# Two PSUM tiles for the halves of an expert's first product, and half an expert's weights loaded ahead of the gathers

## The chip, the cores and the metric

One core of a Trainium2 chip runs the kernel. The metric is the device time of one execution in microseconds. A core has five engines with queues of their own: TensorE (PE in the profile; its weight loads are PEld), VectorE (DVE), ScalarE (ACT), GpSimd (POOL) and SyncE (SP). Sixteen DMA engines move data between HBM and the on-chip memory SBUF. They take work from several queues: q1 is fed by SyncE, q0 by GpSimd. PSUM is the memory that TensorE writes its products to[...].

## The reference

Eight batches of attention with local and global tokens give an array x of 4352 rows and 512 columns. A mixture of experts follows: each row goes to the expert with the largest gate logit, each of eight experts keeps at most 80 rows, those with the largest gates, and only those rows of the output are not zero.

```python
x = np.ascontiguousarray(attn_out.transpose(0, 2, 1, 3)).reshape(B * S, H * D)
...
logits = x @ w_gate
expert_idx = np.argmax(logits, axis=1)
...
for e in range(E):                       # E = 8, D = 512, F = 1024
    tok_idx = np.where(expert_idx == e)[0]
    if len(tok_idx) > capacity:          # capacity = 80
        gw = gate_w[tok_idx]
        tok_idx = tok_idx[np.argpartition(-gw, capacity)[:capacity]]
    h = np.maximum(x[tok_idx] @ w1[e], 0.0)
    out[tok_idx] = gate_w[tok_idx, None] * (h @ w2[e])
```

## The kernel before

The program has a hand-written order on every engine. It runs in three stages.

**Attention.** A loop over sixteen half batches (`q`, L670) computes the attention and writes x, in bf16 and with each row's gate beside it, to the DRAM tensor `x_scr`. SyncE issues those writes (`Ld`, L553). Weights of the experts are loaded on the way by GpSimd, which converts them from fp32 to bf16 in the transfer. `load_w(e, parts)` (L606) loads an expert's weights in four parts of 512 KB as written: parts 0 and 1 are the two halves of the first matrix `w1sb`, parts 2 and 3 those of the second, `w2sb`. Experts 0 to 4 and half of expert 5 are issued inside the loop. `NRES` is 3, so `NRES + 2` is expert 5, `NRES + 3` is 6 and `NRES + 4` is 7.

**Routing.** After the loop SyncE writes the zeros of the whole output (`zeros`, L623, 17 pieces of 512 KB). Then comes, on GpSimd, the rest of expert 5's weights (L815). VectorE finds each expert's threshold and from it the list `idx` of the rows to keep (L876). TensorE runs matmuls that nobody reads meanwhile (`warm`, L635). Then GpSimd issues eight indirect gathers, one per expert, that fetch the kept rows from `x_scr` into `xg` (L880), and behind them, in its queue, the weights of experts 6 and 7 (L883).

**Experts.** For each expert (L924) TensorE does, in this order: four transposes of the next expert's gathered rows (`fx`, L888); the first product of this expert (`fh`, L896), in two halves of 16 matmuls each; the second product of the expert before (`fy`, L907), 8 matmuls of 512 columns. ScalarE empties each half of the first product with a relu (L905). VectorE and ScalarE each scale a half of the second product with the gates, and GpSimd scatters the 80 rows to the output (L917).

In `fh` both halves are written to one PSUM tile from `psO`:

```python
def psO(name):
    return ps.tile([P, 2, 512], FP32, tag="O", bufs=2, name=name)
...
h2_ps = psO(f"h_ps{e}")
for half in range(2):
    h_ps = h2_ps[:, half, 0:4 * cap].rearrange("p (f j) -> p f j", f=4)
```

Such a tile is two banks wide, and half 0 lies in the first bank, half 1 in the second. There are two buffers under the tag "O". The framework adds waits between engines by tile: a write to a tile waits for earlier reads of it.

Of the kernel before, what the change touches and what calls it, by code (L numbers as in the profile page):

```python
# [23 lines left out]
NRES = 3  # L24
# [56 lines left out]
def kernel(  # L81
# [18 lines left out]
    E = moe_w_gate.shape[1]  # L100
# [5 lines left out]
    cap = int(moe_capacity)  # L106
# [20 lines left out]
    def psO(name):  # L127
        return ps.tile([P, 2, 512], FP32, tag="O", bufs=2, name=name)
# [477 lines left out]
    def load_w(e, parts):  # L606
        for k in parts:
            if k < 2:
                nc.gpsimd.dma_start(out=w1sb[e][:, 2 * k:2 * k + 2],
                                    in_=moe_w1[e, 256 * k:256 * k + 256].rearrange("(c p) f -> p c f", p=P))  # L610
            else:
                k -= 2
                nc.gpsimd.dma_start(out=w2sb[e][:, 4 * k:4 * k + 4],
                                    in_=moe_w2[e, 512 * k:512 * k + 512].rearrange("(p c) f -> p c f", c=4))
# [20 lines left out]
    def warm(n):  # L635

        w_ps = psS([P, 512], FP32, "w_ps")
        for _ in range(n):
            nc.tensor.matmul(out=w_ps[:], lhsT=onesb[:], rhs=w1sb[0][:, 0, 0:512], start=True, stop=True)  # L639
# [30 lines left out]
    for q in range(NQ):  # L670
# [95 lines left out]
        if q < 4 * NRES:  # L766
            e, k = divmod(q, 4)
# [43 lines left out]
    for e in range(NRES + 2, E):  # L811
        if e > NRES + 2:
            w1sb[e] = w2pool.tile([P, 4, FF], BF16, name=f"w1sb{e}")
        w2sb[e] = w2pool.tile([P, 8, DF], BF16, name=f"w2sb{e}")
    load_w(NRES + 2, (2, 3))  # L815
    rpool = ctx.enter_context(tc.tile_pool(name="route", bufs=1, reuse_waits="tile"))
    xg = [rpool.tile([cap, XW], FP32, name=f"xg{e}") for e in range(E)]
    for e in range(E):
# [60 lines left out]
    for e in range(E):  # L879
        nc.gpsimd.indirect_dma_start(out=xg[e][:], out_offset=None, in_=x_dram.ap(),  # L880
                                     in_offset=bass.IndirectOffsetOnAxis(ap=idx[:, e:e + 1], axis=0),
                                     bounds_check=N - 1, oob_is_err=False)
    for e in range(NRES + 3, E):  # L883
        load_w(e, (0, 1, 2, 3))
    warm(16)
    xTs, hTs = {}, {}

# [7 lines left out]

    def fh(e):  # L896
        hTs[e] = rpool.tile([P, 8, cap], BF16, tag="fhT", bufs=2, name=f"fhT{e}")
        h2_ps = psO(f"h_ps{e}")
        for half in range(2):
            h_ps = h2_ps[:, half, 0:4 * cap].rearrange("p (f j) -> p f j", f=4)  # L900
            for f in range(4):
                for cc in range(4):
                    nc.tensor.matmul(out=h_ps[:, f, :], lhsT=w1sb[e][:, cc, 512 * half + f:512 * half + 512:4], rhs=xTs[e][:, cc, :],
                                     start=(cc == 0), stop=(cc == 3))
            nc.scalar.activation(out=hTs[e][:, 4 * half:4 * half + 4, :], in_=h_ps, func=AF.Relu, scale=1.0)  # L905
# [18 lines left out]
    for e in range(E):  # L924
        if e + 1 < E:
            fx(e + 1)
        fh(e)
        if e:
            fy(e - 1)
# [37 lines left out]
```

The softmax here doesn't subtract the row's maximum and nothing guards it: scores larger than these inputs give would overflow.

## Time and profile before

| | us |
|---|---|
| median of 3 runs | 281.66 |
| lowest, highest | 279.4, 283.12 |
| span of the profiled execution | 281.7 |
| TensorE busy | 232.1 |
| first gather issued by GpSimd | 230.18 |
| first transpose of gathered rows | 236.78 |
| last scatter issued | 275.86 |

The page gives, for the whole span, the busy time of each engine, then the span in 40 slices, the DMA queues, a chain of waits and the costliest groups of instructions. Each instruction carries the line of the kernel that it comes from. For a change in one stage the answers of the trace by window tell more than the page: who waited for whom between two times, the instructions in order of time, and the DMA queues' share in that stretch. In a timeline line the first number is the start, the second how long the row lasts, then engine, line, operation, out<-in and shapes; in square brackets stand the idle time ahead of it and what ended it. Three slices' worth of numbers of the page frame the stage in question: the memory traffic between 211 and 239 us is 236 to 418 GB/s, between 239 and 268 us 144 to 214, and 47 after that.

### The profile page before, as it was taken

How to read it: one execution, taken by the hardware profiler on the slowest of the kernel's cores; microseconds unless marked ns; L12 is line 12 of the kernel's file. 1: busy time of each engine (PE TensorE's matmuls, PEld its weight loads, DVE VectorE, ACT ScalarE, POOL GpSimd, SP SyncE). 2: the span in 40 equal slices, each digit the busy share in tenths (PEclk: the TensorE clock that was granted, in tenths of full speed). 3: DMA queues.
4: the chain of work that ended last, by engine and by line, in shares of the span. 5: the costliest groups of instructions: out<-in, count | busy, mean ns of one | idle time of the engine just before them, and what ended most of it. 6: DMA issues, size and time to landing. Idle time of an engine off the chain costs nothing.

```text
span 281.7 us, 9676 instructions
## 1 busy us (share of the span) xinstructions
PE 232.1 (82%) x4029; PEld 161.6 (57%) x4029; DVE 146.3 (52%) x450; ACT 137.5 (49%) x238; POOL 158.6 (56%) x215
## 2 busy tenths in 40 slices
PE   8776649999999999999998999979779792598880
PEld 3355537677577676676676677658234352455550
DVE  2647404454554467769168576696879740011210
ACT  3637058669569569569568576450500000123230
POOL 6719409668677776786683987884600027812221
PEclk9999658999999999999999999997999996589998
DMA  7899598969789899999999889969999999899511
GB/s 244 213 299 196 125 342 209 246 189 201 159 215 247 146 254 244 197 261 198 182 261 196 228 164 163 221 122 171 292 273 236 324 418 387 154 213 214 144 47 47
DMA packets 70924, 60.85 MB, mean 216 GB/s; under 512 B 49248, under 2 KB 53600, under 8 KB 70880
## 3 DMA queue, kind: packets, MB, share of 16 engines
q1 hardware_dynamic: 62608, 41.01, 51.5%
q0 software_dynamic: 7840, 18.80, 37.1%
q8 instruction: 31, 0.51, 0.8%
q10 hardware_dynamic: 432, 0.43, 0.4%
q14 instruction: 13, 0.11, 0.1%
HBM read 62.35 MB, written 14.70 MB: 273 GB/s over the span
## 4 chain that ended last, share of the span: by engine, by line
PE 31%; DMA 25%; issue 13%; DVE 10%; ACT 8%; POOL 6%; SPq 4%; POOLq 1%; ACTq 0%; DVEq 0%
PE o_ps L408 7%; DMA x_scr<-xgb 6%; DMA out_dram<-zt 5%; DMA qkb<-in_k_l_dram 5%; PE o_ps L395 5%; DVE xn L416 4%; PE T_ps L308 4%; ACT qkT L311 4%; DMA w1sb<-in_q_g_dram 4%; PE x_ps L443 3%; PE og L427 3%; PE lt_ps L465 3%; DMA vg<-in_v_g_dram 3%; ACT eL L366 2%; POOL out_dram L917 2%
## 5 line engine op out<-in xcount | busy, mean ns | idle before, releaser
L374 POOL TENSOR_TENSOR eL<-eL,band 128x512 f32<-128x512 f32 x30 | 38.8, 1293 | 36.3 <-ACT eL L366 36.2
L311 ACT COPY qkT<-T_ps 128x1024 f16<-128x1024 f16 x32 | 32.5, 1018 | 34.5 <-PE T_ps L308 29.9
L408 PE MATMUL o_ps<-vb,eL 128*64 128x65 f32 x1024 | 45.3, 234 | 0.0
L408 PEld LDWEIGHTS o_ps<-vb,eL 128*64 128x64 f32 x1024 | 36.5, 143 | 9.9 <-issue 6.0
L366 ACT ACTIVATE eL<-l_ps 128x512 f32<-128x512 f32 x64 | 34.9, 600 | 13.9 <-PE l_ps L361 13.9
L158 ACT CAST qkr<-qkb 128x1024 f16<-128x1024 f32 x27 | 28.7, 1064 | 9.6 <-DMA qkb<-in_q_l_dram 8.6
L905 ACT ACTIVATE fhT<-h_ps 128x320 bf16<-128x320 f32 x16 | 6.9, 432 | 48.8 <-remote 37.8
L443 PE MATMUL x_ps<-misc,xn 128*128 128x128 f32 x128 | 20.9, 286 | 8.3 <-DVE xn L416 8.3
L308 PE MATMUL T_ps<-ident,qkr 128*128 128x128 f16 x256 | 21.2, 229 | 7.1 <-ACT qkr L158 5.6
L320 POOL COPY kO<-qkT 128x512 f16<-128x512 f16 x31 | 18.5, 623 | 13.3 <-ACT eg L509 6.8
L639 PE MATMUL w_ps<-w1sb,onesb 128*128 128x512 bf16 x110 | 25.1, 379 | 0.0
L880 POOL DMA_INDIRECT xg<-x_scr,idx x8 | 7.8, 973 | 28.3 <-DMA out_dram<-zt 26.2
L416 DVE TENSOR_TENSOR xn<-o_ps,rec 128x512 f32<-128x512 f32 x32 | 22.1, 692 | 2.1
L415 DVE RECIPROCAL rec<-o_ps 128x8 f32<-128x8 f32 x32 | 6.5, 204 | 32.0 <-PE o_ps L408 32.0
L308 PEld LDWEIGHTS <-qkr 128*128 128x128 f16 x256 | 15.3, 102 | 10.9 <-ACT qkr L158 6.9
L917 POOL DMA_INDIRECT out_dram<-y,idx x8 | 7.4, 930 | 24.0 <-ACT y L915 24.0
L395 PE MATMUL o_ps<-vg,eG 32*128 32x65 f32 x512 | 19.8, 277 | 0.3 <-DMA vg<-in_v_g_dram 0.2
L443 PEld LDWEIGHTS x_ps<-misc,xn 128*128 128x128 f32 x128 | 13.4, 140 | 11.4 <-DVE xn L416 7.3
L454 POOL CAST xb<-xn 128x1024 bf16<-128x1024 f32 x16 | 16.6, 1036 | 4.5 <-DVE xn L416 4.5
L395 PEld LDWEIGHTS o_ps<-vg,eG 32*128 32x128 f32 x512 | 17.2, 186 | 3.3 <-issue 2.2
L224 POOL COPY vb<-vb 64x1040 f32<-64x1040 f32 x16 | 16.7, 1045 | 3.5 <-DMA vb<-in_v_l_dram 3.5
L225 POOL COPY vb<-vb 64x1040 f32<-64x1040 f32 x16 | 17.2, 1077 | 0.9
(148 smaller groups left out, 445.2 us busy)
## 6 DMA issues: line engine op xcount, KB each, us to landing
out_dram<-zt SPq DMA_DIRECT2D x17, 512.0 KB, 9.2
qkb<-in_q_l_dram SPq DMA_DIRECT2D x16, 512.0 KB, 5.8
qkb<-in_k_l_dram SPq DMA_DIRECT2D x16, 512.0 KB, 6.4
vb<-in_v_l_dram SPq DMA_DIRECT2D x48, 128.0 KB, 5.6
w2sb<-in_moe_w_dram POOLq DMA_DIRECT2D x12, 512.0 KB
w1sb<-in_moe_w_dram POOLq DMA_DIRECT2D x10, 512.0 KB
x_scr<-xb SPq DMA_DIRECT2D x8, 514.0 KB, 5.4
vb<-in_moe_w_dram POOLq DMA_DIRECT2D x6, 512.0 KB
```

Of the source, the lines that this page charges most:

```text
L158: cp(out=qkr[q][:, t].rearrange("p i g d -> p g i d"), in_=qkb[q % 2][:, t])
L225: nc.gpsimd.tensor_copy(out=v[64:128, 5:9], in_=v[64:128, 0:4])
L308: nc.tensor.transpose(out=T_ps[:, i].rearrange("x a p -> x (a p)"), in_=qkr[q][:, t, i].rearrange("p g d -> p (g d)"), identity=ident16[:, :])
L311: cp(out=dst, in_=T_ps[:].rearrange("x i a p -> x a p i"))
L320: (nc.gpsimd if q or a else nc.vector).tensor_copy(out=kO[q % 2][:, a], in_=qkT[q % 2][:, a, 576:1088].rearrange("x (u w y) -> x u w y", w ...
L366: nc.scalar.activation(out=eL[:], in_=l_ps[hh][:], func=AF.Exp, scale=scale)
L374: eng.tensor_tensor(out=eL[:], in0=eL[:], in1=band[:].rearrange("p t i -> p (t i)"), op=ALU.mult)
L395: nc.tensor.matmul(out=s["o"][h][:, u, :], lhsT=s["eG"][32 * r:32 * r + 32, 128 * u:128 * u + 128], rhs=vg[b % 2][32 * r:32 * r + 32, qd, ...
L408: nc.tensor.matmul(out=o[64 * odd:64 * odd + 64, u, :], lhsT=s["eL"][h][:, 64 * t:64 * t + 64], rhs=v[:, 5 * odd + u, h, :], start=False, ...
L416: nc.vector.tensor_tensor(out=s["xn"][:, :, 64 * h - 64:64 * h + 64].rearrange("p u (h d) -> p h u d", h=2), in0=o2[:, :, :, 0:64], in1=re ...
L443: nc.tensor.transpose(out=x_ps[:, 128 * u:128 * u + 128], in_=s["xn"][:, u, 128 * j:128 * j + 128], identity=identf[:, :])
L639: nc.tensor.matmul(out=w_ps[:], lhsT=onesb[:], rhs=w1sb[0][:, 0, 0:512], start=True, stop=True)
```

## The change

Two edits, both in the last two stages.

The halves of an expert's first product get a PSUM tile each. The tiles come from the same two buffers, of which each half uses the first bank, so half 0 of every expert is in one buffer and half 1 in the other. It is meant to let TensorE write the second half while ScalarE still reads the first.

Parts 0 and 1 of expert 6's weights, its first matrix, are issued by GpSimd with the rest of expert 5's, ahead of the eight gathers, and no longer behind them. It is meant to put this transfer into an earlier stretch, so that less is left to load while the experts are computed.

```diff
@@ -813,6 +813,7 @@
         w2sb[e] = w2pool.tile([P, 8, DF], BF16, name=f"w2sb{e}")
     load_w(NRES + 2, (2, 3))
+    load_w(NRES + 3, (0, 1))
     rpool = ctx.enter_context(tc.tile_pool(name="route", bufs=1, reuse_waits="tile"))
...
@@ -880,8 +881,8 @@
                                      bounds_check=N - 1, oob_is_err=False)
-    for e in range(NRES + 3, E):
-        load_w(e, (0, 1, 2, 3))
+    load_w(NRES + 3, (2, 3))
+    load_w(NRES + 4, (0, 1, 2, 3))
     warm(16)
...
@@ -895,9 +896,8 @@
         hTs[e] = rpool.tile([P, 8, cap], BF16, tag="fhT", bufs=2, name=f"fhT{e}")
-        h2_ps = psO(f"h_ps{e}")
         for half in range(2):
-            h_ps = h2_ps[:, half, 0:4 * cap].rearrange("p (f j) -> p f j", f=4)
+            h_ps = psO(f"h_ps{e}{half}")[:, 0, 0:4 * cap].rearrange("p (f j) -> p f j", f=4)
             for f in range(4):
```

## The prediction

> **What bounds the kernel now.** I read the page first, for the span (281.7 us) and the slices, then the chain of waits. From 186 us on the chain names mostly "issue", GpSimd and one long DMA, so it does not say what paces the end. I went to the waits of the last 46 us, then to the timeline there.
>
> The page's costliest groups carry a hint: the relu that empties the first product sat idle 48.8 us before its sixteen runs, almost all of it before one of them.
>
> ```profile
> L905 ACT ACTIVATE fhT<-h_ps 128x320 bf16<-128x320 f32 x16 | 6.9, 432 | 48.8 <-remote 37.8
> ```
>
> Waits from 236 to 283 us. The columns are: who waited, for whom, us in total, times, longest. TensorE waits for the relu once per expert.
>
> ```profile
> ACT fhT L905 <- PE h_ps L903: 11.0, 9, 1.3
> PEld L903 <- issue: 9.0, 8, 3.5
> PE h_ps L903 <- ACT fhT L905: 8.2, 8, 3.3
> ```
>
> The timeline of one middle expert shows the shape of that wait.
>
> ```profile
> 257.25 0.74 PE L903 MATMUL h_ps<-fxT,vb 128*128 128x80 bf16 x16
> ...
> 258.20 0.42 ACT L905 ACTIVATE fhT<-h_ps 128x320 bf16<-128x320 f32 x1
> ...
> 258.67 0.73 PE L903 MATMUL h_ps<-fxT,vb 128*128 128x80 bf16 x16 [0.68 <-ACT fhT L905]
> ...
> 259.24 1.90 PE L910 MATMUL y_ps<-qkb,fhT 128*80 128x512 bf16 x8
> ...
> 260.97 0.31 PE L891 MATMUL xT_ps<-identbf,xg 80*128 80x80 bf16 x4
> ```
>
> The second half of the first product starts when the relu of the first half ends (258.20 + 0.42 = 258.62, start 258.67), though it writes other columns. The next expert's first half starts at 261.12, so the period is 3.87 us. After the last gather TensorE is the pacing engine: DVE and ACT do under 1.5 us per period, GpSimd one scatter.
>
> The first expert is worse.
>
> ```profile
> 237.71 1.27 PE L903 MATMUL h_ps<-fxT,w1sb 128*128 128x80 bf16 x16
> ...
> 241.83 0.44 ACT L905 ACTIVATE fhT<-h_ps 128x320 bf16<-128x320 f32 x1 [37.77 <-remote]
> 242.32 1.22 PE L903 MATMUL h_ps<-fxT,w1sb 128*128 128x80 bf16 x16 [3.35 <-ACT fhT L905]
> ```
>
> Its first half ends at 238.98, the relu starts 2.85 us later, and no view says what released it ("remote"). I can't explain this; I carry it as an unknown.
>
> Stages by window (PEclk, DMA share and GB/s are the last three columns): the clock is at half through this time.
>
> ```profile
> 242.02:245.43 3.41, 2.56 (x36) 2.43 (x36) 0.33 (x1) 1.13 (x3) 3.29 (x6) 0.50 0.98 182
> 245.43:248.84 3.41, 3.38 (x22) 2.17 (x22) 0.00 (x0) 0.44 (x1) 0.00 (x0) 0.50 1.12 217
> 248.84:252.26 3.42, 2.75 (x43) 2.03 (x42) 0.71 (x2) 0.94 (x3) 0.99 (x1) 1.00 1.04 210
> ```
>
> DMA, asked by window: the first line is 206 to 222 us, the second and third 222 to 234, the last 242 to 263.
>
> ```profile
> q0 software_dynamic: 944, 2.50, 79.4%
> ```
> ```profile
> q1 hardware_dynamic: 1392, 4.97, 101.9%
> ...
> q0 software_dynamic: 2, 0.00, 0.0%
> ```
> ```profile
> q0 software_dynamic: 1680, 4.28, 106.4%
> ```
>
> Weights (q0) fill the engines until 222 and again from 242 to 263. Between, the zeros for the output (q1) fill them alone, while q0 is empty. That empty stretch is where the moved half expert will go.
>
> **What the Trainium skill says.** "PSUM — Partial Sum Buffer", PSUM bank collisions: guard PSUM by bank and quadrant. The halves lie in different banks (L900), so the wait above is the tile's, not the memory's; the trace agrees so far as the wait ends with the relu. "TensorE: Matmul & The Clock Gate", Part 1: the clock falls to half after an idle window of about 3.4 us and returns after a busy one. Agrees: TensorE's last warming matmul ends at 232.4, the next work is at 236.78, the clock is 0.50 from 235.19, it stays so over a window busy for 2.56 of 3.41 us and returns after one busy for 3.38. "DMA: Bandwidth & Descriptors", Queues, rings and completion order: engines take turns between rows at packet granularity. Agrees roughly: from 206 to 222 q0 moved 944 packets, q1 1109.
>
> **The change part by part.**
>
> *Separate tiles, experts 2 to 7 (full clock).* Sixteen matmuls issue in 259.24 − 258.67 = 0.57 us. The first half issues until 257.25 + 0.57 = 257.82, so TensorE stands 258.67 − 257.82 = 0.85 us. Check: four transposes 0.14, two halves 1.14, the second product 7 × 0.217 + 0.22 = 1.74 ((1.90 − 0.379)/7 is the spacing), plus 0.85, is 3.87. Without the wait the period is 3.02. The new wait, first half on the previous expert's first relu (two buffers in rotation), asks for a relu that ended over 2 us before: nothing. The relus move behind the second half and the second product, which hide them. Six experts: 5.1 us.
>
> *Separate tiles, experts 0 and 1 (half clock).* If the odd 2.85 us recurs, expert 1's first half must still wait until 242.27 for the relu of expert 0, since it reuses its buffer; but expert 0's second half and four transposes are done by then. So expert 1 starts at 242.3 and not 243.61, and its own stall (244.66 to 245.46) goes: the second product of expert 0 starts at 244.4 and not 246.49. At half clock its eight take about 0.43 each (twice 0.217), so it ends near 247.8; expert 2's halves then run partly at half clock, to 249.6, and the second product of expert 1 to 251.3, against 250.94 + 0.57 + 1.74 = 253.25 before. Gain there 1.9 us, expert 2 included. With experts 3 to 7, 5 × 0.85 = 4.25: 6.15 us, all on the path, since the last scatter (275.86) and the 5.8 us to the end follow the last product.
>
> *Clock.* With no stall inside it, the window 242.02 to 245.43 may count as busy. The clock would return 3.4 us sooner and save half of that, up to 1.7 us. The windows run free, so I count on about half: 0.8.
>
> *The moved loads.* On GpSimd two descriptor writes, 1.57 us (the pair at 240.10), go to 203.8, ahead of a memset that is wanted at 222.9; GpSimd idles 26.2 us there, so nothing. After the gathers 1.57 us of issue is gone. On the DMA engines a quarter of q0's eight late parts (21 us for 4.28 MB) is 5.1 us of work, moved to 222 onwards, beside the zeros. Taking turns with 16 engines, 512 packets of 213 ns (106.4% of 16 × 21 us over 1680) beside as many of 140 ns (101.9% of 16 × 12 us over 1392) last 11.3 us, to about 233. The zeros end about 5 us later, near 244.5; the scatters behind them are not ready before 246. The last weights, busy to 263 before, end near 260 or 261; their product is now wanted at about 266. Hidden, then, as is the rest of this part.
>
> *What it can cost.* The first gather issues at 230.18 and its rows are used at 236.78. Behind weights to 233 on the same queue it may come later: 0 if the usual 6.6 us cover it, at most 2.8 us (233 − 230.2). I take 0.3, since before, too, the gathers' packets began only near 234 (q0 has 2 packets from 222 to 234).
>
> Sum: 281.7 − 6.15 − 0.8 + 0.3 = 275.0 us.
>
> **The rivals.**
>
> (a) *More*: the 2.85 us does not recur, or the clock returns two windows sooner. Expert 1 then starts near 240.1; up to 2 us of start and 1.7 to 3.4 of clock come on top: 271 to 273. For it: nothing on the page ties the wait to the kernel's own work. Against it: unexplained is not absent. Below 271 the last weights (260 to 261) bound the last product.
>
> (b) *Gathers late*: the half expert holds the gathers 1.5 to 2.8 us, and the clock stays low a window more (1.7): 6.15 − 1.5 to 4.5 leaves 277 to 280. For it: q1 alone uses 101.9% of the engines there, no room is free. Against: packets take turns, and the moved part is only 512.
>
> (c) *Not faster*: the zeros don't share as fairly, and the gathers stand behind weights and zeros both, until 245 and not 235.5: +9.5 − 6.15, 285. Or the last weights bind at both ends and the gain is eaten: 281. Against: the shares of 206 to 222.
>
> **How the numbers follow.** Forecast (273 to 277) 0.55, (a) 0.17, (b) 0.2, (c) 0.08. The range holds the forecast, (a) and most of (b): 271.0 to 279.0. Faster by 2% means under 276.0: (a), and 0.48 of the forecast's 0.55 because its low gain of 5.7 us is the boundary: 0.65. Slower by 2% (over 287.3) only at the far end of (c): 0.03. Rest 0.32.
>
> **What would show it.** Right: the wait "PE h_ps L903 <- ACT fhT L905" gone but for expert 1; the period of an expert near 3.0 us; the first gathered rows used within 0.5 us of 236.8; q0 busy from 222 to about 233; no DMA named before the last products. Wrong: transposes of experts 0 to 2 waiting long for gathered rows, a second product waiting for weights, the clock low past 249, or a period near 3.9.

## The result, and the profile after

| | before | after |
|---|---|---|
| median, us | 282.39 (4 runs, 279.4 to 283.68) | 271.01 (4 runs, 269.68 to 278.75) |
| span of the profiled execution, us | 281.7 | 267.9 |
| first gather issued | 230.18 | 226.77 |
| first transpose of gathered rows | 236.78 | 232.83 |
| last scatter issued | 275.86 | 262.06 |

The ratio is 0.9615, 95% interval 0.9495 to 0.9735; executions lengthened by a disturbance are left out of the ratios. The prediction was 275.0 us, 271.0 to 279.0: the time lies inside the range by a hundredth of a microsecond, which is luck, and in rival (a).

The spans differ by 13.8 us. Of that, 3.4 us lie ahead of the first gather (230.18 against 226.77), where nothing on the path was changed; in the kernels below, the same point falls anywhere from 226.8 to 238.2 us, for the most part later where the mean granted clock of the whole execution is lower (226.8 us at 0.955, 238.2 at 0.910). So I measure the changed stage from its own start: from the first gather to the last scatter, 45.7 us before and 35.3 us after. That stretch does not follow the mean clock: one kernel, e8 and e11 below, needs 42.6 us in it at 0.957 and 42.3 at 0.911. The 10.4 us between before and after are what has to be explained.

The relu's group on the page of after: the idle time ahead of it now ends with TensorE, not "remote".

```profile
L905 ACT ACTIVATE fhT<-h_ps 128x320 bf16<-128x320 f32 x16 | 6.7, 430 | 36.3 <-PE h_ps L903 36.2
```

The waits of after from 222 to 270 us (who waited, for whom, us in total, times, longest).

```profile
ACT fhT L905 <- PE h_ps L903: 36.2, 3, 35.3
...
POOL out_dram L917 <- ACT fhT L905: 10.1, 2, 9.8
...
DVE y L914 <- DMA out_dram<-y,idx: 4.2, 1, 4.2
...
PE y_ps L910 <- DMA w2sb<-in_moe_w_dram: 0.4, 1, 0.4
```

TensorE's wait for the relu, 8.2 us before, is no longer in the list. Three waits are new: GpSimd ahead of the first scatter, 9.8 us long, for something other than its rows; VectorE for a buffer of `y` that a scatter must have emptied; TensorE for the last weights. The timeline of after, at the first expert and at a middle one:

```profile
234.11 2.34 PE L903 MATMUL h_ps<-fxT,w1sb 128*128 128x80 bf16 x32
...
235.75 0.44 ACT L905 ACTIVATE fhT<-h_ps 128x320 bf16<-128x320 f32 x1 [35.30 <-PE h_ps L903]
...
242.78 1.31 PE L903 MATMUL h_ps<-fxT,qkb 128*128 128x80 bf16 x32
...
243.93 1.90 PE L910 MATMUL y_ps<-w2sb,fhT 128*80 128x512 bf16 x8
...
245.66 0.31 PE L892 MATMUL xT_ps<-identbf,xg 80*128 80x80 bf16 x4
...
245.81 1.31 PE L903 MATMUL h_ps<-fxT,vb 128*128 128x80 bf16 x32
```

The two halves are now one unbroken row of 32 matmuls, and from one expert to the next it is 245.81 − 242.78 = 3.03 us, where it was 3.87. And expert 0's relu starts while the second half still runs: the odd wait of 2.85 us is not there.

The clock by window (the third column from the end): one window at half, where before it was four (235.19 to 248.84). How much of this belongs to the change is taken up with e10.

```profile
230.17:233.58 3.41, 0.32 (x4) 0.18 (x4) 0.32 (x1) 0.00 (x0) 2.50 (x4) 1.00 1.02 416
233.58:236.99 3.41, 3.13 (x48) 3.13 (x49) 0.57 (x2) 0.88 (x2) 2.80 (x4) 0.50 1.03 415
236.99:240.41 3.42, 3.42 (x59) 2.61 (x58) 0.68 (x3) 0.95 (x3) 3.23 (x6) 1.00 1.03 412
```

The end of after, by the timeline.

```profile
250.34 0.97 POOL L917 DMA_INDIRECT out_dram<-y,idx  x1 [9.76 <-ACT fhT L905]
...
259.04 1.02 PE L910 MATMUL y_ps<-w2sb,fhT 128*80 128x512 bf16 x4 [0.40 <-DMA w2sb<-in_moe_w_dram]
...
259.58 1.05 DVE L914 TENSOR_SCALAR y<-y_ps,xg 80x256 f32<-80x256 f32 x2 [4.17 <-DMA out_dram<-y,idx]
...
262.06 0.91 POOL L917 DMA_INDIRECT out_dram<-y,idx  x1 [0.30 <-issue]
```

The first scatter goes out at 250.34, though the first product was scaled by 240.8. A relu is named as its releaser, but the one next to it in time (249.82 us) is of a later expert, whose rows this scatter does not carry. The zeros go to the same output and must be written first, and the queues say when those ended. The queues of after from 240 to 248 us (packets, MB, share of 16 engines), and from 248 to 249 us:

```profile
q0 software_dynamic: 381, 1.22, 73.9%
q1 hardware_dynamic: 270, 0.97, 31.5%
```
```profile
q1 hardware_dynamic: 4, 0.01, 2.4%
```

q1, the zeros, still takes a third of the engines between 240 and 248 us; its last four packets run between 248 and 249 us, and from 249 us it has none. A scatter at 250.34 fits that. The rows show no semaphore, so the reading rests on the timing, and on five more kernels below in which the first scatter follows the last zeros in the same way.

VectorE's wait of 4.2 us ends at 259.58, when the first scatter, issued at 250.34, lands and frees its buffer; the eight scatters of after take 2.6 to 9.1 us from issue to landing. The zeros are long over by then. What ends just ahead of it, at 259.04, is the load of the last weights, which GpSimd issued ahead of the scatters on its own queue; e7 and e9 below show the same.

### The profile page after: what moved, and what is told of

Its sections match the earlier page's. It is cut to its first block, busy times and chain, and to the rows that moved or that the text cites. A ratio compares the mean times of both kernels' runs of the same rounds, so it can differ in the third digit from the quotient of the medians.

```text
span 267.9 us, 9673 instructions
## 1 busy us (share of the span) xinstructions
PE 229.2 (86%) x4025; PEld 159.2 (59%) x4029; DVE 145.9 (54%) x450; ACT 137.2 (51%) x238; POOL 158.0 (59%) x215
## 4 chain that ended last, share of the span: by engine, by line
PE 42%; DMA 21%; DVE 11%; ACT 11%; issue 6%; POOL 5%; SPq 2%; POOLq 1%; ACTq 0%; DVEq 0%
DMA out_dram<-zt 12%; PE o_ps L408 8%; PE o_ps L395 5%; ACT qkT L311 4%; PE T_ps L308 4%; DVE xn L416 4%; PE y_ps L910 4%; ACT eL L366 4%; PE og L427 4%; PE h_ps L903 3%; DMA qkb<-in_q_l_dram 3%; PE x_ps L443 3%; PE lt_ps L465 3%; DMA w1sb<-in_k_g_dram 2%; DMA xg<-x_scr,idx 2%
## 5 line engine op out<-in xcount | busy, mean ns | idle before, releaser
L408 PEld LDWEIGHTS o_ps<-vb,eL 128*64 128x64 f32 x1024 | 35.9, 140 | 10.3 <-issue 5.9
L639 PE MATMUL w_ps<-w1sb,onesb 128*128 128x512 bf16 x106 | 26.0, 393 | 0.3 <-issue 0.2
L639 PEld LDWEIGHTS <-onesb 128*128 128x128 bf16 x110 | 10.6, 101 | 13.7 <-issue 3.2
```

The lines of the kernel that those rows point to most:

```text
L408: nc.tensor.matmul(out=o[64 * odd:64 * odd + 64, u, :], lhsT=s["eL"][h][:, 64 * t:64 * t + 64], rhs=v[:, 5 * odd + u, h, :], start=False, ...
```

## The experiments

The kernels ran in three groups, one after another within a group, and each group on another chip: e1, e2, e3 and e5 on the first, e6 to e9 on the second, e10 to e13 on the third. For before and after themselves the chip is not known. This table is read from the timelines (us); "late" is the time from the end of expert 0's first half to the start of its relu, and "the stage" below is its last column.

| kernel | first gather | to first transpose | late | first gather to last scatter |
|---|---|---|---|---|
| before | 230.18 | 6.60 | 2.86 | 45.7 |
| e3 before, again | 229.17 | 5.83 | 3.01 | 45.4 |
| e2 the move alone | 230.18 | 6.43 | 3.33 | 45.4 |
| e1 the tiles alone | 238.24 | 6.47 | 3.29 | 39.2 |
| e5 after, more unread matmuls | 232.30 | 6.25 | 3.95 | 40.3 |
| e8 before, altered reads | 227.62 | 6.67 | 0.38 | 42.6 |
| e10 before, a third time | 230.49 | 6.34 | 0.38 | 42.4 |
| e11 before, altered reads | 236.31 | 6.52 | 0.38 | 42.3 |
| e7 the tiles alone, again | 231.71 | 6.31 | 0.38 | 38.1 |
| after | 226.77 | 6.06 | 0.38 | 35.3 |
| e6 after, again | 229.74 | 6.31 | 0.38 | 35.4 |
| e9 after, most zeros left out | 227.32 | 2.63 | 0.38 | 32.9 |
| e13 after, eight buffers for y | 234.38 | 6.17 | 0.38 | 34.5 |
| e12 after, a whole expert ahead | 229.65 | 9.02 | 0.38 | 42.7 |

The last column runs from issue to issue.

### The parts one by one: e1, e2, e3

e1 is the tiles alone:

```diff
-        h2_ps = psO(f"h_ps{e}")
         for half in range(2):
-            h_ps = h2_ps[:, half, 0:4 * cap].rearrange("p (f j) -> p f j", f=4)
+            h_ps = psO(f"h_ps{e}{half}")[:, 0, 0:4 * cap].rearrange("p (f j) -> p f j", f=4)
```

> The kernel before with a PSUM tile for each half, and all of expert 6's weights still behind the gathers. Theory A (the wait between the halves is the cost, the moved weights are hidden anyway): the period of an expert falls from 3.87 to about 3.02 us, the wait of TensorE for the relu goes, and the time falls by 6 to 10 us to 272 to 276; the last quarter of the weights lands later than with the move (near 260 to 263 us) and may hold the last product by up to 2 us. Theory B (the moved weights do much of it, by clearing the DMA engines while the first experts run): only the six stalls of 0.85 us go, about 5 us, to 277, and the odd wait of 2.85 us ahead of expert 0's first relu is still there.

Measured: 278.39 us (274.26 to 285.25, 5 runs), ratio 0.9746 (0.9608 to 0.9884); the stage 39.2 us, against 45.4 and 45.7 of before.

e2 is the move alone:

```diff
     load_w(NRES + 2, (2, 3))
+    load_w(NRES + 3, (0, 1))
...
-    for e in range(NRES + 3, E):
-        load_w(e, (0, 1, 2, 3))
+    load_w(NRES + 3, (2, 3))
+    load_w(NRES + 4, (0, 1, 2, 3))
```

> Both halves again in one PSUM tile, half of expert 6's weights ahead of the gathers. Theory A: within 1.5 us of the kernel before (281 to 284), period 3.87 us, eight waits of TensorE for the relu. Theory B: 4 to 5 us faster than before (277 to 279), and the first relu starts within 0.5 us of the end of expert 0's first half, since the transfer that disturbed it has moved.

Measured: 285.33 us (283.24 to 287.14, 4 runs), ratio 1.0118 (1.0012 to 1.0224); the stage 45.4 us. Alone, the move gains nothing, if it does not cost a little: with the old period no product waits for the last weights. The zeros hold the first scatter here too, until 251.87, 1.5 us after its rows are ready; with the old period that costs nothing at the end.

e3 is before, unchanged, on the same chip.

> The kernel before, unchanged, profiled a second time. If the 2.85 us between the end of expert 0's first half and its relu belongs to the program, it is there again, with nothing that ends it. If it is an accident of one execution (theory C), the relu starts within 0.5 us, and TensorE is held 0.9 us there as in the other experts. The two cases tell how much of the 13.8 us between the two profiled spans is chance: 2.5 us of it with theory C, and the start of the gathers (230.18 in one, 226.77 in the other) should then vary by a few us too.

Measured: 282.25 us. The odd wait is there once more (timeline of e3):

```profile
236.70 1.27 PE L903 MATMUL h_ps<-fxT,w1sb 128*128 128x80 bf16 x16
...
240.97 0.44 ACT L905 ACTIVATE fhT<-h_ps 128x320 bf16<-128x320 f32 x1 [38.22 <-remote]
241.46 1.23 PE L903 MATMUL h_ps<-fxT,w1sb 128*128 128x80 bf16 x16 [3.50 <-ACT fhT L905]
```

It is also in e1 and e2, of which each has one of the two edits. So for a moment it looked as if only both edits together removed it.

### Is the odd wait the clock's or the queue's? e5

e5 is after with 32 unread matmuls and not 16 behind the gathers (`warm(32)`), so that TensorE is not idle for long before the gathered rows come.

> The changed kernel with 32 and not 16 unread matmuls between the list of rows and the first gathered rows: TensorE is then busy to about 232.7 of 232.8 us. Theory D (the clock, not the DMA queue, sets the end now): no window at half clock there, the 3.4 us of work done at half clock takes half, 1.5 us faster than the changed kernel (about 269.5). Theory E (the DMA queue sets the end: zeros hold the scatters to 250.3 and the last weights land at 259): the products of all experts are 1.5 us earlier, the waits for the zeros, the last weights and the first scatter grow by as much, and the time is the changed kernel's within 0.5 us (270.5 to 271.5).

Measured: 278.66 us (275.08 to 280.4, 4 runs), ratio 0.9783 (0.9637 to 0.9929). Neither theory held. The clock by window:

```profile
239.34:242.75 3.41, 1.90 (x40) 1.68 (x41) 0.33 (x1) 0.00 (x0) 2.80 (x4) 1.00 1.03 415
242.75:246.16 3.41, 1.52 (x24) 1.52 (x24) 0.33 (x1) 0.97 (x3) 3.18 (x6) 0.50 1.03 416
246.16:249.58 3.42, 3.42 (x19) 1.89 (x17) 0.00 (x0) 0.67 (x2) 0.00 (x0) 0.50 1.08 295
```

The matmuls did keep the clock at full speed while the rows were fetched, but the odd wait came all the same, 3.95 us long, at full clock and with both edits in place; and the idle time that it made then cost the clock two windows later on. So the half clock does not make the wait, and the two edits do not take it away. The same execution has such a wait a second time, while GpSimd issues the first scatters back to back (timeline of e5); that expert's period is 263.57 − 259.08 = 4.49 us and not 3.03, a part of why the stage took 40.3 us.

```profile
262.81 0.77 ACT L905 ACTIVATE fhT<-h_ps 128x320 bf16<-128x320 f32 x2 [2.04 <-remote]
```

### The second chip: e6, e7, e8

e6 is after, unchanged; e7 the tiles alone, unchanged from e1.

> The changed kernel once more, on the same chip as the next three. The other kernels' first relu of expert 0 comes 2.5 to 3.6 us after the records of its products end (before twice, move alone, tiles alone, longer warming); in the one profile of the changed kernel it came 0.4 us after. Theory F (a matter of the execution, more likely than not, for any of these kernels): here it is late in this profile too and the time from first gather to last scatter, 35.3 us in the first profile, is then 38 to 39; times spread over 270 to 279 us. Theory G (the change itself takes it away): 0.4 us again, 35.3 us again, times 269 to 272.

Measured: 272.05 us (268.47 to 274.24, 6 runs), ratio 0.9695 (0.9622 to 0.9768); late by 0.38 us, the stage 35.4 us. The result repeats.

> A tile for each half, no moved weights, again, beside the changed kernel on one chip. Theory A (the moved weights take the end off the DMA queue and are worth 1 to 2 us): 1 to 2 us slower than the changed kernel. Theory G (with the weights behind the gathers the first relu is late, with the move it is not): 3.5 to 5 us slower, with the late relu in the profile and two more windows at half clock. Theory H (the move is worth nothing): same time as the changed kernel within 1 us.

Measured: 276.91 us (271.83 to 283.91, 6 runs), ratio 0.9777 (0.968 to 0.9873); late by 0.38 us, though e1, the same kernel, had 3.29. The waits of e7 from 240 to 276 us show what limits it now:

```profile
DVE y L913 <- DMA out_dram<-y,idx: 6.5, 1, 6.5
...
PE y_ps L909 <- DMA w2sb<-in_moe_w_dram: 2.4, 1, 2.4
```

With the tiles alone TensorE reaches the last expert 2.4 us before its weights. In after that wait is 0.4 us. So the move, worth nothing alone, is worth 38.1 − 35.4 = 2.7 us behind the tiles (e7 and e6, on one chip). The times by themselves do not separate these two kernels, since their intervals overlap; the stage and its waits do. VectorE's wait ends at 267.17, 0.5 us after TensorE's wait for the last weights (266.63), though the first scatter left at 247.66: it took 19.4 us to land. In e12 below, where all weights are there before the scatters leave, each lands in 2.6 or 2.7 us.

e8 is before with every second unread matmul reading the third quarter of expert 0's first matrix, so that TensorE meets that load's semaphore early:

```diff
-        for _ in range(n):
-            nc.tensor.matmul(out=w_ps[:], lhsT=onesb[:], rhs=w1sb[0][:, 0, 0:512], start=True, stop=True)
+        for i in range(n):
+            nc.tensor.matmul(out=w_ps[:], lhsT=onesb[:], rhs=w1sb[0][:, 2 * (i % 2), 0:512], start=True, stop=True)
```

> The kernel before, with every second unread matmul reading the other half of expert 0's first weights, so that TensorE has met the wait on those weights' transfer long before, and expert 0's first product waits for no transfer but the gathered rows. In five executions the late relu was released within 0.3 us of a transfer on the semaphore which that wait names. Theory I (the wait on that semaphore holds it): the relu follows the product within 0.5 us. Theory J (it has nothing to do with it): 2.5 to 3.6 us late, as in both profiles of the kernel before.

Measured: 277.89 us, late by 0.38 us. The edit looked like the cure; but on this chip no kernel was late, and the unchanged before had not been profiled on it. Hence e10.

### What do the zeros cost? e9

e9 is after without the 13 pieces of zeros that are written behind the attention (`zeros(17)` left out): only four of the 17 pieces of the output are zeroed, so what it writes is incomplete.

> The changed kernel without the last 13 of the 17 pieces of zeros (6.8 MB of the output are not written). Theory E (the DMA queue sets the end: zeros hold the scatters and delay the weights): the first gathered rows come 1 to 2 us after their issue sooner, the scatters follow the products one by one, no product waits for the last weights, 2 to 4 us faster than the changed kernel. Theory K (TensorE's products set the end alone): within 1 us of the changed kernel. If the late relu comes from full DMA engines, it is not there.

Measured: 268.83 us (267.83 to 276.48, 4 runs), ratio 0.9614 (0.953 to 0.9698); the stage 32.9 us. The first rows are used 2.63 us after the first gather's issue, not 6.06: 3.4 us of the gathers' time is the zeros. But the end does not gain as much, 2.4 us, because other things bind there (waits of e9 from 222 to 270 us):

```profile
DVE y L913 <- DMA out_dram<-y,idx: 6.0, 1, 6.0
PE y_ps L909 <- DMA w2sb<-in_moe_w_dram: 2.3, 1, 2.3
```

The first scatter leaves at 241.23, no longer held, and still takes 16.4 us to land, so that VectorE gets its buffer at 257.73, 0.5 us after TensorE gets the last weights (257.22). As in after and e7, the scatter lands with the last of the weights ahead of it on GpSimd's queue. So VectorE's wait does not come from the zeros' hold on the scatters.

### Once more the odd wait: e10, e11

e10 is before, unchanged, and e11 is e8's kernel again.

> The kernel before once more, unchanged, beside the run with the altered reads. In question is the late start of expert 0's first relu (2.9 to 4.0 us behind the end of its first half in five profiles, 0.38 us in five others). Theory J (it goes with the execution or the chip and not with the kernel): late or not late as in the next run of this call, whatever that is; 280 to 283 us if late, 277 to 279 us if not. Theory I (the reads of the unread matmuls decide): late here, 2.9 to 3.3 us, and not in the next run. First gather to last scatter: 45.4 us if late, 42.6 us if not.

> The kernel before, in which every second unread matmul ahead of the gathers reads a slice of the third quarter of expert 0's weights instead of the first, so that TensorE meets that weight load's semaphore before expert 0 needs it. Theory I: expert 0's first relu starts 0.4 us after its first half ends, although it starts 2.9 to 3.3 us late in the unchanged kernel of this call; first gather to last scatter 42.6 us, against 45.4 us. Theory J: both kernels of this call show the same, late or not.

Measured: 280.49 us and 286.26 us; late by 0.38 us in both, the stage 42.4 and 42.3 us. The unchanged kernel is not late here (timeline of e10):

```profile
238.66 1.27 PE L903 MATMUL h_ps<-fxT,w1sb 128*128 128x80 bf16 x16
...
240.30 0.44 ACT L905 ACTIVATE fhT<-h_ps 128x320 bf16<-128x320 f32 x1 [36.14 <-PE h_ps L903]
...
240.79 1.23 PE L903 MATMUL h_ps<-fxT,w1sb 128*128 128x80 bf16 x16 [0.86 <-ACT fhT L905]
...
244.66 1.89 PE L910 MATMUL y_ps<-w2sb,fhT 128*80 128x512 bf16 x8
```

The altered reads change nothing: 42.3 and 42.6 us with them, 42.4 without. The wait goes with the group: all four kernels on the first chip had it, none on the second or third. Since each group had a chip of its own, the runs cannot tell a chip's habit from a passing condition. The wait is worth about 45.5 − 42.4 = 3.1 us, of which 2.5 are the wait and the rest more time at half clock.

### More of the same, and the new end: e12, e13

e12 moves all four parts of expert 6 ahead of the gathers:

```diff
-    load_w(NRES + 3, (0, 1))
+    load_w(NRES + 3, (0, 1, 2, 3))
...
-    load_w(NRES + 3, (2, 3))
```

> The kernel after with all four parts of expert 6's weights ahead of the gathers, not two: 1024 packets of weights beside the zeros, not 512. The forecast's term for the gathers: by its sharing of the engines (213 ns and 140 ns a packet, 16 engines) 1024 packets beside as many of zeros last 22.6 us from 222 us, to 244.6 us, past the first gather at 230.2 us plus its usual 6.3 us. If the queue's order holds the gathers back, the first transpose comes 10 to 14 us after the first gather, not 6.3 us, and the time is 275 to 280 us. Rival (packets of the two rings of descriptors, or of the same queue, pass one another): the first transpose stays within 1 us of 6.3 us, the last weights land 3 to 5 us sooner, and the time is 269 to 272 us, as after, since the zeros then end later and the scatters wait for them.

Measured: 281.12 us (277.22 to 282.68, 4 runs), beside 280.99 us of before (277.29 to 285.64, 7 runs); no interval is on record. The whole gain of the change is lost. The gathers are late by 2.7 us, less than the first theory said; the rest is the mechanism that I had put with the rival, and far larger than it said. Parts 2 and 3 go in packets of twice the size (in before 224 packets for 0.85 MB from 248 to 252 us, beside 219 for 0.42 MB from 244 to 246), so e12 moves 768 packets and not 1024. Timeline of e12:

```profile
261.98 3.62 PE L909 MATMUL y_ps<-w2sb,fhT 128*80 128x512 bf16 x16
263.72 0.99 POOL L916 DMA_INDIRECT out_dram<-y,idx  x1 [21.25 <-issue]
265.01 0.96 POOL L916 DMA_INDIRECT out_dram<-y,idx  x1 [0.30 <-issue]
...
266.61 0.48 DVE L913 TENSOR_SCALAR y<-y_ps,xg 80x256 f32<-80x256 f32 x1 [5.10 <-DMA out_dram<-y,idx]
...
272.37 0.92 POOL L916 DMA_INDIRECT out_dram<-y,idx  x1 [0.30 <-issue]
```

TensorE is done at 265.6 and never waits for weights, but no scatter leaves before 263.72, 34.1 us after the first gather, and the eight scatters then take 1.24 us each. Where the zeros were at that time, DMA of e12 from 248 to 260 us:

```profile
q0 software_dynamic: 578, 1.54, 65.3%
q1 hardware_dynamic: 517, 1.86, 41.4%
```

and from 262 to 263 us, the last stretch with zeros in it:

```profile
q1 hardware_dynamic: 2, 0.00, 1.1%
```

In steps of one microsecond, the last zeros run before 239 us in e7 and 243 in e10, where nothing is moved (7 and 12.5 us after the first gather; the other five such kernels lie between), before 249, 253, 257, 251 and 256 in after, e6, e13, e2 and e5, with two parts moved (21 to 24 us), and before 263 in e12, with four (33 us). In the last six kernels the first scatter goes out 0.7 to 1.3 us later, at 250.34, 253.90, 258.03, 251.87, 256.87 and 263.72. So the zeros hold the scatters, and each two parts hold the zeros by about 10 us.

e13 is after with eight buffers for `y` in place of six (`bufs=8`), and with the altered reads, which by e11 do nothing.

> The kernel after with eight buffers for the scaled product y, not six, and with the altered reads of the unread matmuls. In the kernel after VectorE waits 4.2 us for a buffer of y that the first scatter must land to free (about 259.5 us), and the last two scatters go out at 261 and 262 us. If that wait sets the end, the last scatter comes 1 to 2 us sooner after the first gather (33.5 to 34.5 us, not 35.3) and the time is 270 us against 271 to 272 us. Rival (GpSimd's scatters are held by the zeros and each by the one before, so that the buffers only move the wait): the wait of VectorE is gone, the last scatter stays at 35.0 to 35.4 us after the first gather, and the time is within 0.5 us of the kernel after.

Measured: 273.75 us (269.99 to 276.69, 4 runs), ratio 0.9685 (0.9548 to 0.9822). VectorE's wait for the first scatter is gone, and the stage is 34.5 us against 35.3 and 35.4. The wait for a buffer did set the end, by 0.8 us; but the time cannot be told from that of after, since the start of the gathers, by chance 234.38 us here, varies by more. No version measured that writes the whole output beats after.

## Why the prediction was right, and where not

Its mechanism held, and the time fell into the range, but by 0.01 us, and in the rival (a) and not in the forecast. Step by step, each number from the first gather on. To compare like with like I use e10, the before without the odd wait, against after: 42.4 to 35.3, 7.1 us.

| step | predicted, us | measured, us |
|---|---|---|
| period of an expert | 3.02 | 3.03 |
| experts 2 to 7, stall gone | 5.1 | 4.7, after 0.4 given back to the last weights |
| experts 0 and 1 and the clock | 1.05 + 0.8 | 2.8 in this pair, 1.9 to 2.8 in others |
| the odd wait of expert 0 | 0, recurs | about 3.1 to 3.3, absent |
| the move | 0, hidden | 0 alone, 2.7 behind the tiles |
| its cost to the gathers | 0.3 | not seen (6.06 and 6.31, against 5.83 to 6.67) |
| zeros end | near 244.5, hidden | near 249, first scatter 250.34; no cost of this hold seen |
| last weights | 260 to 261 | 259.0, wait of 0.4 |
| from the last product's end to the last scatter | no change | 0.6 longer, the wait for a buffer of `y` |

*Experts 2 to 7.* From the start of the first second product to the end of the last: 271.50 − 244.66 = 26.84 us in e10, 260.06 − 237.88 = 22.18 us in after. The tile's wait was the whole of the stall, as the prediction argued from 258.62 and 258.67. The relus moved behind the second half cost nothing. Of the stage's 7.08 us these are 4.66; 2.78 lie in experts 0 and 1 and 0.28 in an earlier first transpose, and 0.64 are lost again behind the last product.

*Experts 0 and 1, and the clock.* From the first transpose to the first second product: 7.83 us in e10, 5.05 in after, 5.18 in e6. Predicted without expert 2 (1.9 − 0.85 = 1.05) and with 0.8 of clock it was 1.85. A part of this pair's 2.8 is chance: in e10 TensorE waits 1.26 us for the second expert's rows, in after 0.71. In e11, which does not wait there, the stretch is 7.12. The clock was the term taken too low. The half clock ends 7.5 us after the first transpose in e10, 7.6 in e8 and 8.0 in e11, but 4.2 in after and 4.9 in e6: 2.6 to 3.9 us sooner, of which half is saved, 1.3 to 1.9 us (an estimate from these ends): about the "up to 1.7" of the prediction, which then counted half of it. The count of windows alone, two in e10 and e6, three in e11, one in after, depends on where the windows happen to begin.

*The odd wait.* This is the step that made most of the error. The prediction kept it as recurring, though its rival (a) said that nothing on the page ties it to the kernel's own work; e10, unchanged and without it, shows that this was so. Before and after were profiled, by chance, one with it and one without, so the pair of profiles flatters the change: 10.4 us in the stage, where the kernel's own part is 7.1. The second chip, where no profiled kernel had the wait, gives a ratio of 0.9695, 8.5 us between the medians; that is the better figure for the change, though its interval overlaps the first. Put on 281.7 us it makes 273.1 us, an estimate at the low end of the forecast.

On the first chip, where every profiled kernel had the wait, the tiles alone shortened the stage from 45.4 to 39.2 us: 6.2 to 6.5 us, where the prediction's sum for that very case, worked out from the half-clock rows, was 6.15.

*The move.* "Hidden" was right as long as the old period, or the odd wait, let the weights keep ahead: e2 gains nothing, and e1 shows no wait for weights. It was wrong for the case that came. The prediction saw the limit itself ("below 271 the last weights bound the last product") but did not draw the conclusion that in rival (a) the move is then worth something. Here the two edits are not additive: 4.3 us for the tiles (e10 to e7) and 0 for the move alone (e2, with the odd wait; without it the move alone was not run) make 7.1 together. The sign "no DMA named before the last products" did not come true.

*The zeros.* The term was mis-sized: 244.5 predicted, 14.3 us after the first gather, against 22 measured. The prediction let the zeros share the engines with the moved weights only ("the zeros end about 5 us later"), and forgot that zeros which end later then meet the weights issued behind the gathers (from 236.7 us) as well, and share again; the lines from 240 to 248 us are that second meeting. The 270 packets of zeros in them, at the prediction's own 140 ns, are 2.4 us of all sixteen engines (an estimate); they took almost 9 us. The prediction also gives the moved half two sizes, 5.1 us and 512 packets of 213 ns, which are 6.8 us. By the Trainium skill ("DMA: Bandwidth & Descriptors", Queues, rings and completion order) the engines take turns between queue rows by packets. The trace of e12 agrees where both queues are full, with 578 packets against 517 from 248 to 260 us; it was the count of packets in the way that was too small. In after the hold on the scatters costs nothing that the runs show: the 0.8 us that e13 takes back is the wait for a buffer, which ends with the last weights in e7 and e9 too. In e12 it costs everything, though not as rival (c) had it: the gathers come only 2.7 us late, and it is the scatters that stand behind the zeros.

## What to carry to other kernels

A wait between two halves that never touch the same memory is worth looking for in the tile they share; its worth is the stall times the repetitions, until the next transfer binds, and an edit that only brings that transfer forward is worth nothing before and something after. Moving a load into a full stretch of the DMA engines is paid by what is there already, so look at who waits for that, and expect the cost to jump once its slack is used up: two moved parts and two more each held the zeros by about 10 us, the first two at no cost seen, while with the next two the stage grew by 7.4 us (2.7 of them late gathers). A small transfer that is issued behind large ones on the same queue may land only with them: the scatters took 2.6 us alone and up to 19.4 behind weights. Before the difference of two profiles is put down to an edit, profile the unchanged kernel again: here a wait that comes and goes made up 3 of 10 us.

## What the runs showed that I had not expected

The odd wait itself. In five of fourteen profiles expert 0's relu starts 2.9 to 4.0 us after the last record of the matmuls that it needs, and in the other nine 0.38 us after. TensorE's semaphore updates for that half come as late as the relu, and in e1 and e5 those of several groups of matmuls come within 0.2 us of each other. In all five the relu starts 1.7 to 2.0 us after the last gather instruction has ended on GpSimd; in eight of the other nine it starts before that end or with it. The second such wait of e5 falls among the first scatters, also indirect transfers that GpSimd issues back to back. So bursts of these are the suspect, but no run without the burst was made on the first chip, and other executions have the same bursts and no wait. Whatever holds the updates was not found: not the clock (e5), not the reads of the unread matmuls (e8, e10, e11), not either edit. It went with the group of runs, and so with the chip or with a condition of that time.

The clock comes back without a fully busy window. By the windows of e10, TensorE was busy for 2.83 of 3.42 us at half clock and had full clock in the next; in before 2.56 of 3.41 had not been enough. In e5 a window with 1.90 of 3.41 lost it. So the prediction's "idle window" and "busy one" need not be wholly idle or wholly busy.

```profile
240.90:244.32 3.42, 2.83 (x43) 2.71 (x43) 0.32 (x1) 0.87 (x2) 3.21 (x6) 0.50 0.95 203
244.32:247.73 3.41, 2.96 (x41) 2.06 (x39) 0.71 (x2) 1.06 (x3) 1.49 (x3) 1.00 1.11 202
```

Moved weights delay the zeros by more than their own work: from 7 to 12.5 us after the first gather to 21 to 24 with two parts, and to 33 with four, though by the prediction's 213 ns a packet 512 packets are 6.8 us of all sixteen engines. The last of the zeros are thin, a few packets in a microsecond, as in the two single rows above.
